# An attention and MLP kernel: for one unit per group, a DMA adds the first bit piece to the second, and one product per block falls away

## The chip, the core and the metric

The kernel runs on one core of one Trainium2 chip. The core has five engines with queues of their own, worked through in order: TensorE (PE, matmuls), ScalarE (ACT, activation functions), VectorE (DVE), GpSimd (POOL) and SyncE (SP, which issues DMAs). They meet through semaphores only. Data lie in SBUF and, for matmul results, in PSUM, each with 128 partitions; PSUM has eight banks of 512 fp32 values per partition. Sixteen DMA engines move data beside them.

The metric is device time in microseconds of one execution.

## The reference

```python
D, H, S, F = 640, 32, 2048, 1536                 # Dh = 20
xn = layernorm(x)
qkv = xn @ wqkv                                  # split into q, k, v of 32 heads
p = softmax(q @ k.T * Dh ** -0.5)                # 32 heads, 2048 x 2048 each
s = (p @ v) @ wo
h = gelu(layernorm(xn) @ w1)                     # then shifted by 1, -1, 2, -2 rows, by quarters of D
x1 = xn + shifted(h) @ w2
b = x1 + gelu(layernorm(x1) @ w3) @ w4
out = x + s * silu(b)
```

The costly part are the exponentials of the softmax: 32 heads of 2048 x 2048 scores, 134 million in all.

## The kernel before, in words

**Groups.** The 32 heads are worked in eight quads of four heads, and the 2048 queries in four chunks of 512: 32 groups (`attn_quad`). A group runs over 16 key tiles of 128 keys. For each key tile PE makes the scores of the four heads, two heads to a score tile of 128 keys x 1024 (two PSUM banks). Scores are made in one of two forms (`score_pair`): as row products, one matmul per head with four heads side by side in the rows of the array (line 1459), or as column products, four matmuls per head in the columns, over queries of one head with the other heads' rows at zero (line 1472). The planner decides the form of most tiles.

**Exponentials on two engines.** Most score tiles go through ACT (`exp_act`, line 1518), which writes the exponentials in bf16 into a tile of PT, a pool of 7. For the key tiles listed in `BLK`, half the score tiles take another way (`score_both`): DVE multiplies and adds (line 1540) so that the result, as a 16-bit integer, is the bit pattern of a rough exponential in bf16. It is kept in U, a pool of two buffers. One block is two key tiles, and its part in U is 2048 columns wide; a unit is one or two blocks, up to 4096 columns.

**Bit pieces.** `block_bits` refines that rough value. It takes the pattern four times, with 0, 32, 64 and 96 added to the integer (`EXP_B`): piece 0 is U itself, pieces 1 to 3 are written into SS, a pool of three buffers, by DVE (line 1442) or, for piece 3 of most units, by POOL (line 1440, a 32-bit integer add). PE multiplies all four with the values of the keys and adds up in PSUM (line 1451): one product of four matmuls per block and piece. Pieces 0 and 1 have weight 1 and take the values VA; pieces 2 and 3 have the weight 181/256 and take scaled values VP. The four matmuls of a product are one per head, with 22 columns of weights (20 values, a column of ones for the sum, one of zeros) and 512 queries.

The products of all key tiles of a group, those of PT (line 1312) and those of the pieces, add up in one PSUM bank. `ends` counts them, so that the first starts and the last ends the sum. DVE then takes the result out (line 1561), POOL normalises, and a transposing DMA and four more put it into HBM.

**Units.** `UNITS` says after which key tile of a group each unit's scores stand. Groups have two, four or five blocks (`ND`), so one to three units; the first unit of a group always holds blocks 0 and 1. The last of the 32 groups is made in another way (`last_half`) and has no such unit.

**What sets the order.** The program records tasks with the data that they read and write. The order of all of them, on all engines, is written out as one long string, `TABLE`: `follow` reads it, takes each task in turn onto its engine's queue, and gives out PSUM banks and PT tiles by the string's digits. It was made by a search elsewhere, with assumed durations; at run time only the order of each queue and the semaphores count. Tasks with `lock` are DVE operations in SBUF and POOL tasks; a POOL task waits for the last DVE task of that kind before it.

Everything else (projections of keys, queries and values, the MLP with its normalisations, the output projection) is fitted between the groups by the same string; its matmuls are mostly on line 684 (`mm_tile`).

Of the kernel before, what the change touches and what calls it, by code (L numbers as in the profile page):

```python
# [57 lines left out]
class Planner:  # L58
    def __init__(self):
# [15 lines left out]
        self.dma_lat0 = 1950.0  # L75
# [375 lines left out]
U8 = mybir.dt.uint8  # L451
# [15 lines left out]
class Cfg:  # L467
# [5 lines left out]
    def __init__(self, S=2048, D=640, H=32, F=1536):  # L473
# [34 lines left out]
        self.DT = False  # L508
        self.QS = False
# [46 lines left out]
        self.W7 = (0, 1)  # L556

# [56 lines left out]
class Gen:  # L614
# [76 lines left out]
    def build(self, plan_only=False):  # L691
        nc, pl = self.nc, self.pl
        with contextlib.ExitStack() as es:
# [12 lines left out]
                                for y in range(x + 1, 7) if x not in p and y not in p])  # L706
            pl.kind("SR", "B", [(2 * (k > 1), p + q) for k, p in enumerate(pairs) for q in pairs if not set(p) & set(q)])
# [95 lines left out]
    def alloc_persistent(self):  # L803
# [19 lines left out]
        self.PT = self.alloc("PT", [7, 1024], BF16)  # L823
# [36 lines left out]
    def load_inputs(self):  # L860
        cfg = self.cfg
        T, A = self.T, self.A
        X = self.xn
        xv = self.aps["A_x"][0].rearrange("(n p) d -> p n d", p=128)
        for n0 in range(0, cfg.NT, 2):
            n1 = n0 + 2
            T("sp", C_SP, lambda e, n0=n0, n1=n1: e.dma_start(X[:, n0:n1, :], xv[:, n0:n1, :]),
              writes=[A("xn", n) for n in range(n0, n1)], is_dma=True, nbytes=(n1 - n0) * 128 * cfg.D * 2,
              name=f"ld_x{n0}")
# [3 lines left out]
    def ln_tiles(self, tag, tiles, dst_of, dst_atoms_of, ve_out=None):  # L873
# [389 lines left out]
    def attn_quad(self, quad):  # L1263
# [9 lines left out]
        for qc in range(NQC):  # L1273
# [4 lines left out]
            if col:  # L1278
                T("sp", 2600, lambda e, qc=qc, gb=gb: [e.dma_start(self.QM[32 * i:32 * i + 32, gb, i, :],
                                                                 QT[32 * i:32 * i + 32, b, 512 * qc:512 * qc + 512]) for i in range(4)],  # L1280
                  reads=[A("QT", b, qc), A("QTa", b, qc)], writes=[A("QM", gb)], is_dma=True, nbytes=131072, name=f"qm{quad}_{qc}",
# [6 lines left out]
            done, total = [0], sum(5 if x[0] == "b" else 1 for x in seq)  # L1288
# [35 lines left out]
    def last_half(self, quad, qc, half, gb):  # L1324
# [40 lines left out]
        for x, kt in enumerate(ks):  # L1365
# [9 lines left out]
            for unit in at.get(x, []):  # L1375
# [3 lines left out]
                for m, kx in enumerate(unit):  # L1379
# [4 lines left out]
                      reads=[sa], writes=[A("U", ub, m)], name=f"uh{half}_{kx}", rel=hs, cls=-1 - half, due=self.at(self.nact, f"u{quad}"))  # L1384
                for v in range(4):
                    if v == 0:
                        dst, dsta = U[:, ub, :], [A("U", ub, m) for m in range(len(unit))]
                    else:
# [5 lines left out]
                          reads=[A("U", ub, m) for m in range(len(unit))], writes=dsta, name=f"s_h{half}_{unit[0]}_{v}", cls=-2 * half, lock=True,  # L1394
# [25 lines left out]
    def block_bits(self, quad, qc, blocks, ends):  # L1420
# [8 lines left out]
        halves = [A("U", ub, k) for k in range(2 * len(blocks))]  # L1429
        for v in range(4):  # L1430
# [13 lines left out]
            for n, (j, kts) in enumerate(blocks):  # L1444
# [17 lines left out]
    def score_pair(self, b, qc, kt, a, hs, sa, gb):  # L1462
        T, A = self.T, self.A
        me = []
        def fn(e):
            for jj in range(2):
                out = self.bank(hs.slots[jj])
# [3 lines left out]
                for c in range(4):  # L1471
# [5 lines left out]
                    writes=[sa], name=f"sc{self.tag}_{kt}_{a}", mode=int(gb is None), part=a + 1, flex=gb is not None, cls=-1, acq=("S", hs)))  # L1477
# [46 lines left out]
    def score_both(self, b, qc, kt, a, quad, r, gb):  # L1524
# [8 lines left out]
        (hs, sa), (hd, da) = self.stile(), self.stile()  # L1533
        for x, (h, ta) in ((a, (hs, sa)), (o, (hd, da))):
            self.score_pair(b, qc, kt, x, h, ta, gb)
        slot = self.exp_act(hs, sa, f"{self.tag}_{kt}_{a}")
        def fnu(e):
# [5 lines left out]
        T("dve", c_dve(1024), fnu, reads=[da], writes=[A("U", ub, at)], name=f"u{quad}_{qc}_{kt}", rel=hd,  # L1543
# [306 lines left out]
    def b_alloc3(self):  # L1850
# [6 lines left out]
        self.y3 = self.alloc("y3", [4, D], BF16)  # L1857
# [4 lines left out]
    def b_w34(self, c0):  # L1862
# [6 lines left out]
        for ch in (c0, c0 + 1):  # L1869
            i = ch % 2  # L1870
            tiles = list(range(4 * ch, 4 * ch + 4))
            tmp = self.ln_tiles(f"ln3_{ch}", tiles, lambda n, ch=ch: y3[:, n - 4 * ch, :], lambda n, ch=ch: [A("y3", n - 4 * ch)])
            self.free(*tmp)
            for bi, n in enumerate(tiles if cfg.DY else ()):
                T("sp", 1350, lambda e, bi=bi: e.dma_start_transpose(y3T[:, :, 128 * bi:128 * bi + 128], y3[:, bi, :]), reads=[A("y3", bi)],
                  writes=[A("y3T", bi)], is_dma=True, nbytes=163840, dlat=100.0, name=f"ty3_{n}", stream=f"ty{n % 4}")
            for kc in range(0 if cfg.DY else KC):
                self.transpose_w(f"y3_{ch}", kc, tiles, lambda n, ch=ch: y3[:, n - 4 * ch, :], lambda n, ch=ch: [A("y3", n - 4 * ch)],
# [16 lines left out]
        for hh in range(2):  # L1895
            hs = slice(hh * HALF, (hh + 1) * HALF)
            T("sp", C_SP, lambda e, hs=hs: e.dma_start(W4[:, :, :], w4src[:, :, hs]),
              writes=[A("W4")], is_dma=True, nbytes=FC * 128 * D, name=f"ld_w4_{c0}_{hh}", stream="w4")
# [19 lines left out]
    r"#9#0$R###%$G$$$^$<$,#(#&#,#6#:#'#;#<#)#$#*#-#i#a$&$-&J&K$.$%#`$'#y#v$(#u$)#x#=#w#>#b#.#?#t$/#@$0#z$1$*#A#{#B#|#_#m#j#d#k$+#n#C#l#o#}#D#E#p$3#F#f$_#G#H"  # L1918
    r"#q#I$K#J#~%((#K$I#L$L#g#M#N#O#P#Q$H$M$J#R#r#S#s$p#$z%${$|$k$$l$m$2$4$5$#%#&$6$N$7#c%$%%$O%&$A$u'$v$q$r$n$=$o#T$}$`$~$a$>$b$8$Q$@$w$x#e$V$?%'#U#V$y%7)$"
    r"s$t$;%-$#W$B$P$C$W#h#X#Y%_'%<#%`$S#Z#[$D%f&&I$c$E$e%D$9%g%=$d$F%2%%.$:%/%8%>%3%0$f%?$g%9%@%1%:%h%i%;%j$T$U%4%)%5%a%b%c$X$Y%6&L$&M(@&N&O%*%+&P&Q&b#&c%C"  # L1920
    r"$Z&d&e%,&f%m$%n#+$[%E%#]#^$]%d%Y'$h%J(%K$i%k%o%l%p%q%O)&g%F%G$j%H%T#%L#2#5%Z%M%I%P%U%N%[%V%]%A%W%^%X%Q%R%S%B%t&%u%v%r%s%w%x%y%{#%|%}%~%e&#&S(&T&U&$&%&"
    r"&&.$&V&W&/&'&0(A&)&X&,)&-&1&2&7#&8)}$&3%z)~#*#'*$&4&9**(*+%*&$*(*%#&:&;*,(&<*5$*')*1#*7(D&5#&6&(*-#*.*4(*2&*/$&Z&&[&]&^+$&o#16&_&p&`&q&r&s&t*6#*O(*0$*"
    r"9#*;*8$*3&@#&=&A&B&C*P(*H(*:$*J#&D']*)&E&i(&j&>)*D*I%&?&k&l&m*K)&n*]'&|$&}&~*^&*T$*M#*N',1*L'#'$'%&u#*U)&v&w*<&x&y*R#*d(*e%*Q'3('4'5&F&G)&z*='6'7*_'''"
# [118 lines left out]
```

## Time and profile before

| | |
|---|---|
| median of 3 runs | 804.62 us (802.0 to 806.14) |
| the profiled execution | 805.04 us, its span 803.3 us |
| PE busy | 777.6 us, 13680 matmuls |
| ACT busy | 766.8 us |
| DVE busy | 717.6 us |
| POOL busy | 328.5 us |
| DMA | 58.25 MB, 30.3% of the DMA engines' span for the main queue |
| granted TensorE clock | 0.99 |

Every line of the profile names a source line, an engine, an operation, the tiles (out<-in, all of them cut from one arena in SBUF, or psum), shape and count. Busy time and mean duration follow, then the idle time of the engine just before, with what ended it (the releaser). PE's busy time is the union of matmuls whose ends are modelled and overlap, so a busy PE is not a PE at its peak; what a matmul costs is better seen from how far apart starts are. PEld is PE's loading of weights, which runs ahead of the matmul. SPq is SP's queue of DMA issues. Stretches are given in us from the span's start.

### The profile page before, as it was taken

What the parts mean: (1) busy time and instruction counts of PE and PEld (TensorE: products, weight loads), DVE (VectorE), ACT (ScalarE), POOL (GpSimd) and SP (SyncE); (2) the same over time, 40 slices, a digit from 0 to 9 for tenths busy, and PEclk for the clock granted to TensorE, in tenths of its full rate; (3) what the DMA queues carried; (4) which work ended last, traced back from release to release, by engine and by line L of the source; (5) the groups of instructions that cost most, each with busy time, mean ns of one, the idle gap of its engine ahead of it and who ended that gap; (6) DMA issues with size and microseconds to landing.
All of it is one profiled execution on the core that took longest, in us unless ns stands there. A gap on an engine that the chain in (4) does not pass through costs nothing.

```text
span 803.3 us, 30126 instructions
## 1 busy us (share of the span) xinstructions
PE 777.6 (97%) x13680; PEld 329.5 (41%) x13680; DVE 717.6 (89%) x934; ACT 766.8 (95%) x796; POOL 328.5 (41%) x201
## 2 busy tenths in 40 slices
PE   7999999999999999999999999999998999999996
PEld 3443333334444433333534444334333444434574
DVE  7878899989999999998999899989888988888866
ACT  6899999999998999999999999999999999998995
POOL 5554334342426426344332453533423343444342
PEclk9999999999999999999999999999999999998998
DMA  5132433342213315423241132324232203123433
GB/s 176 31 107 61 130 90 73 78 90 55 52 20 62 54 45 110 85 57 82 67 109 31 34 84 61 67 52 83 55 91 51 50 14 85 27 62 115 100 103 100
DMA packets 141359, 58.25 MB, mean 73 GB/s; under 512 B 113728, under 2 KB 136432, under 8 KB 141232
## 3 DMA queue, kind: packets, MB, share of 16 engines
q1 hardware_dynamic: 141232, 56.33, 30.3%
q8 instruction: 107, 1.75, 0.9%
q14 instruction: 20, 0.16, 0.1%
HBM read 34.70 MB, written 10.33 MB: 56 GB/s over the span
## 4 chain that ended last, share of the span: by engine, by line
PE 48%; ACT 41%; DVE 8%; DMA 2%; SPq 0%; issue 0%; DVEq 0%
ACT arena L1518 35%; PE psum L684 16%; PE psum L1459 10%; PE psum L1451 8%; PE psum L1312 5%; PE psum L1472 5%; DVE arena L1540 3%; ACT arena L1892 3%; PE psum L1353 2%; DVE arena L1442 1%; DMA arena<-in_B_w_dram 1%; ACT arena L1818 1%; DVE arena L891 1%; DMA arena<-in_A_x_dram 1%; ACT arena L1908 1%; ACT arena L1500 1%
## 5 line engine op out<-in xcount | busy, mean ns | idle before, releaser
L1518 ACT ACTIVATE arena<-psum 128x1024 bf16<-128x1024 f32 x728 | 678.2, 1038 | 18.6 <-PE psum L1459 11.6
L1540 DVE TENSOR_SCALAR arena<-psum 128x1024 uint16<-128x1024 f32 x268 | 325.9, 1219 | 37.7 <-PE psum L1459 33.4
L684 PE MATMUL psum<-arena 128*32 128x320 bf16 (+1 forms) x5808 | 336.2, 332 | 1.7 <-DVE arena L1142 0.9
L1440 POOL TENSOR_TENSOR arena<-arena 128x2048 int32<-128x2048 int32 x61 | 219.6, 3600 | 284.1 <-DVE arena L1442 169.1
L1459 PE MATMUL psum<-arena 32*128 32x512 bf16 x1594 | 189.6, 385 | 10.6 <-ACT arena L1518 6.6
L684 PEld LDWEIGHTS psum<-arena 128*32 128x32 bf16 x5808 | 140.2, 96 | 124.8 <-issue 33.8
L1451 PE MATMUL psum<-arena 128*22 128x512 bf16 x2144 | 183.1, 382 | 0.0
L1442 DVE TENSOR_SCALAR arena<-arena 128x4096 uint16<-128x4096 uint16 (+1 forms) x158 | 170.5, 1100 | 2.2 <-PE psum L1451 1.4
L1312 PE MATMUL psum<-arena 128*22 128x512 bf16 x1448 | 137.9, 384 | 1.5 <-DVE arena L1561 1.3
L1459 PEld LDWEIGHTS psum<-arena 32*128 32x128 bf16 x1594 | 53.2, 91 | 174.0 <-ACT arena L1518 93.2
L1472 PE MATMUL psum<-arena 128*32 128x512 bf16 x1560 | 119.4, 382 | 0.7 <-ACT arena L1518 0.4
L1451 PEld LDWEIGHTS psum<-arena 128*22 128x22 bf16 x2144 | 50.0, 91 | 57.8 <-issue 23.0
L1569 POOL TENSOR_TENSOR arena<-arena 128x512 bf16<-128x512 f32 x30 | 40.9, 1365 | 58.5 <-DVE arena L1442 23.9
L1312 PEld LDWEIGHTS psum<-arena 128*22 128x22 bf16 x1448 | 35.5, 91 | 48.4 <-issue 21.9
L1472 PEld LDWEIGHTS psum<-arena 128*32 128x32 bf16 x1560 | 33.6, 95 | 41.7 <-ACT arena L1518 30.0
L1888 DVE CAST arena<-psum 128x512 bf16<-128x512 f32 x48 | 32.8, 683 | 4.6 <-PE psum L684 4.5
L1188 DVE CAST arena<-psum 128x512 bf16<-128x512 f32 x40 | 27.1, 683 | 1.8 <-PE psum L684 1.5
L891 DVE BATCH_NORM_STATS2 arena<-arena 128x6 f32<-128x320 bf16 x54 | 24.5, 480 | 3.1 <-DMA arena<-in_A_x_dram 3.1
L1730 POOL TENSOR_TENSOR arena<-arena 128x640 bf16<-128x640 bf16 x12 | 16.8, 1400 | 25.6 <-DVE arena L1668 20.0
L1668 DVE SCALAR_TENSOR_TENSOR arena<-psum,arena 128x320 bf16<-128x320 f32 x32 | 15.4, 487 | 11.7 <-PE psum L684 11.3
L1500 ACT ACTIVATE arena<-psum 128x2048 bf16<-128x2048 f32 x13 | 24.5, 1887 | 1.2 <-PE psum L1459 1.2
L1561 DVE STREAM_TRANSPOSE arena<-psum 128x512 f32<-128x512 f32 x31 | 22.1, 712 | 4.1 <-PE psum L1312 1.8
(120 smaller groups left out, 353.3 us busy)
## 6 DMA issues: line engine op xcount, KB each, us to landing
arena<-in_B_w_dram SPq DMA_DIRECT2D x48, 160.0 KB, 2.8
arena<-arena SPq DMA_DIRECT2D x124, 32.0 KB, 2.2
arena<-in_B_w_dram SPq DMA_DIRECT2D x4, 960.0 KB, 5.4
arena<-in_A_x_dram SPq DMA_DIRECT2D x8, 320.0 KB, 6.3
arena<-in_A_x_dram SPq DMA_DIRECT2D x16, 160.0 KB, 2.4
out_dram<-arena SPq DMA_DIRECT2D x16, 160.0 KB, 2.3
heads<-arena SPq DMA_DIRECT2D x120, 20.0 KB, 2.0
arena<-queries SPq DMA_DIRECT2D x28, 80.0 KB
```

The costliest lines, as they stand in the source:

```text
L684: ins = e.matmul(pb[32 * c:32 * c + 32, 0:N], lhsT(k, c), rhs(k, c), start=(k == 0), stop=(stop and k == nk - 1), tile_position=(0, 32 * c))
L891: lambda e, li=li, n=n, hh=hh: e.bn_stats(st[:, li, 6 * hh:6 * hh + 6], xn[:, n, hD * hh:hD * hh + hD]),
L1312: ins = e.matmul(pb[32 * i:32 * i + 22, 0:512], VA[:, ql, kts[i // 2], i, :], PT[:, slots[i // 2][0].slot, 512 * (i % 2):512 * (i % 2) + 512],
L1440: return e.tensor_tensor(dst.bitcast(I32), U[:, ub, 0:w].bitcast(I32), bass.AP(c.tensor, c.offset, [list(c.ap[0]), [0, w // 2]]), op=ALU.add)
L1442: fa if onp else lambda e, v=v, dst=dst: e.tensor_scalar(dst, U[:, ub, 0:w], EXP_B[v], None, op0=ALU.add),
L1451: ins = e.matmul(pb[32 * i:32 * i + 22, 0:512], wv, dst[:, at:at + 512].bitcast(BF16), start=first, stop=final, tile_position=(0, 32 * i))
L1459: return e.matmul(out, self.KT[32 * i:32 * i + 32, b, 128 * kt:128 * kt + 128], self.QT[32 * i:32 * i + 32, b, 512 * qc:512 * qc + 512], s ...
L1472: ins = e.matmul(out[32 * c:32 * c + 32, :], self.KT[:, b, 128 * kt + 32 * c:128 * kt + 32 * c + 32], self.QM[:, gb, 2 * a + jj, :], start ...
L1518: lambda e: e.activation(self.PT[:, hp.slot, :], self.psum[:, 512 * hs.slot:512 * hs.slot + 1024], AF.Exp, scale=cfg.scale),
L1540: ins = e.tensor_scalar(U[:, ub, 1024 * at + 512 * k:1024 * at + 512 * k + w], self.psum[:, 512 * hd.slots[k]:512 * hd.slots[k] + w], a_ex ...
L1569: return e.tensor_tensor(OnT.rearrange("p (k d a) -> p a k d", k=4, a=4), Ob[:, :].rearrange("p (a k d) -> p a k d", a=4, k=4), in1, op=AL ...
L1888: T("dve", c_dve(512), lambda e, h=h, fc=fc, i=i: e.tensor_copy(GT[:, i, fc, :], self.wbank(h)[:, 0:512]), reads=[wa], writes=at, name=f"g ...
```

## The change

For the first unit of each of 31 groups, the `acc` units of `ACC`, POOL issues a DMA that adds U (4096 columns of bf16 in 128 partitions, 1024 KB) onto piece 1 in SS, in SBUF. It waits for U and for piece 1, and the product of piece 1 waits for it. The products of piece 0 are left out for that unit, so three per block remain; `total` counts accordingly. Piece 1 of these units is made by DVE.

PT gets eight tiles instead of seven. The buffer y3 of the MLP's second normalisation holds two row tiles instead of four (`Y2`), and each tile's transposing DMA is recorded right behind its normalisation (`after`) instead of behind all four. The new kind "S2" and the option `US` are not used. Some assumed DMA durations (`dma_lat0`, `dlat`) differ, which changes no instruction. The string `TABLE` is new as a whole: the order of all queues and the choice of row or column form for some scores are others.

```diff
@@ Cfg
+        self.Y2 = True
+        self.NPT = 8
+        self.ACC = {(q, c): (0, 1) for q in range(8) for c in range(4)}
@@ alloc_persistent
-        self.PT = self.alloc("PT", [7, 1024], BF16)
+        self.PT = self.alloc("PT", [cfg.NPT, 1024], BF16)
@@ ln_tiles
                   reads=[A("xn", n), A(tag + "_rs"), A(tag + "_nb", li)], writes=dst_atoms_of(n), name=f"{tag}_norm{n}")
+                if after:
+                    after[li]()
                 continue
@@ attn_quad
-            done, total = [0], sum(5 if x[0] == "b" else 1 for x in seq)
+            done, total = [0], sum(5 - (x[1] in cfg.ACC.get((quad, qc), ())) if x[0] == "b" else 1 for x in seq)
@@ block_bits
-        halves = [A("U", ub, k) for k in range(2 * len(blocks))]
+        halves = [A("U", ub, k, x) for k in range(2 * len(blocks)) for x in range(2)]
+        acc = blocks[0][0] in cfg.ACC.get((quad, qc), ())
...
-            for n, (j, kts) in enumerate(blocks):
+            if acc and v == 1:
+                T("pool", 1000, lambda e, dst=dst: e.dma_start(dst.bitcast(BF16), U[:, ub, 0:w].bitcast(BF16), accum_op=ALU.add, max_dma_last_dim=4096),
+                  reads=halves + dsta, writes=dsta, is_dma=True, nbytes=2 * 256 * w, name=f"acc{quad}_{qc}_{blocks[0][0]}", stream="acc", lock=True)
+            for n, (j, kts) in enumerate([] if acc and v == 0 else blocks):
@@ b_alloc3
-        self.y3 = self.alloc("y3", [4, D], BF16)
+        self.y3 = self.alloc("y3", [2 if cfg.Y2 else 4, D], BF16)
@@ b_w34
-            tmp = self.ln_tiles(f"ln3_{ch}", tiles, lambda n, ch=ch: y3[:, n - 4 * ch, :], lambda n, ch=ch: [A("y3", n - 4 * ch)])
+            ny = 2 if cfg.Y2 else 4
+            yt = lambda n: y3[:, n % ny, :]
+            ya = lambda n: [A("y3", n % ny)]
+            turn = [lambda n=n: T("sp", 1350, lambda e: e.dma_start_transpose(y3T[:, :, 128 * (n % 4):128 * (n % 4) + 128], yt(n)), reads=ya(n),
+                                  writes=[A("y3T", n % 4)], is_dma=True, nbytes=163840, dlat=100.0, name=f"ty3_{n}", stream=f"ty{n % 4}") for n in tiles]
+            tmp = self.ln_tiles(f"ln3_{ch}", tiles, yt, ya, after=turn if cfg.DY else None)
-            for bi, n in enumerate(tiles if cfg.DY else ()):
-                T("sp", 1350, lambda e, bi=bi: e.dma_start_transpose(y3T[:, :, 128 * bi:128 * bi + 128], y3[:, bi, :]), reads=[A("y3", bi)],
-                  writes=[A("y3T", bi)], is_dma=True, nbytes=163840, dlat=100.0, name=f"ty3_{n}", stream=f"ty{n % 4}")
```

More of the change, by code (lines that the diff above doesn't have):

```diff
@@ L706, in build @@
                                 for y in range(x + 1, 7) if x not in p and y not in p])
+            pl.kind("S2", "B", [(2 * (k > 1), p) for k, p in enumerate(pairs)] + [(3, [i, j]) for i in range(7) for j in range(i + 2, 7)])
             pl.kind("SR", "B", [(2 * (k > 1), p + q) for k, p in enumerate(pairs) for q in pairs if not set(p) & set(q)])
@@ L1393, in last_half @@
                           lambda e, v=v, dst=dst, ub=ub, w=w: e.tensor_scalar(dst[:, 0:w], U[:, ub, 0:w], EXP_B[v], None, op0=ALU.add),
-                          reads=[A("U", ub, m) for m in range(len(unit))], writes=dsta, name=f"s_h{half}_{unit[0]}_{v}", cls=-2 * half, lock=True,
+                          reads=[A("U", ub, m, x) for m in range(len(unit)) for x in range(2)], writes=dsta, name=f"s_h{half}_{unit[0]}_{v}", cls=-2 * half, lock=True,
                           due=self.at(self.nact, f"s{quad}"))
```

215 lines of the change are left out of this document (114 added, 101 removed).

## The prediction

> **What bounds the kernel now.** I read the summary first, then the slices, the chain, the groups, the waits and a stretch of the timeline. Engine busy times, and ScalarE (ACT) by slices of 20 us:
>
> ```profile
> PE 777.6 (97%) x13680; PEld 329.5 (41%) x13680; DVE 717.6 (89%) x934; ACT 766.8 (95%) x796; POOL 328.5 (41%) x201
> ...
> ACT  6899999999998999999999999999999999998995
> ```
>
> Two engines look full. The stretch between prologue and tail (columns: PE, weight loads, DVE, ACT, POOL, then clock and DMA share) says how full:
>
> ```profile
> 40.00:780.00 740.00, 726.20 (x12470) 299.52 (x12466) 672.40 (x814) 723.41 (x735) 300.27 (x155) 1.00 0.31 70
> ```
>
> ACT idles 740.0 - 723.4 = 16.6 us in 740 (2.2%). Its instructions are the same in both kernels, so this is what the change can gain there. PE's busy time includes overlapping ends of matmuls; its real room shows in the starts:
>
> ```profile
> 399.36 20.32 ACT L1518 ACTIVATE arena<-psum 128x1024 bf16<-128x1024 f32 x22
> ...
> 400.91 0.60 PE L1451 MATMUL psum<-arena 128*22 128x512 bf16 x8
> ...
> 405.69 0.39 PE L1451 MATMUL psum<-arena 128*22 128x512 bf16 x4
> ...
> 413.47 0.39 PE L1459 MATMUL psum<-arena 32*128 32x512 bf16 x4
> ...
> 420.96 0.82 PE L1451 MATMUL psum<-arena 128*22 128x512 bf16 x12
> ```
>
> (Columns: start, duration, engine, line, count.) Four matmuls more cost (0.82 - 0.39) / 2 = 0.215 us: the price of one product. Four row scores (L1459) take the same 0.39, and some 0.1 more in the gap around them, say 0.43 us. One exponential costs 20.32 / 22 = 0.924 us, the beat of the kernel. The chain and the waits agree on who leads:
>
> ```profile
> PE 48%; ACT 41%; DVE 8%; DMA 2%; SPq 0%; issue 0%; DVEq 0%
> ...
> PEld psum L1459 <- ACT arena L1518: 93.2, 232, 1.0
> ...
> ACT arena L1518 <- PE psum L1459: 11.6, 31, 0.8
> ACT arena L1518 <- PE psum L1472: 3.3, 5, 1.1
> ```
>
> The score loads wait 93.2 us for ACT to free PSUM, ACT waits some 15 us for scores. The two alternate, and ACT leads.
>
> **What goes.** 31 units lose two products each: 62 x 0.215 = 13.3 us of PE. The order of the built program also has 96 fewer column-score matmuls (24 x 0.215 = 5.2 us) and 24 more row-score matmuls (6 x 0.43 = 2.6 us). Together PE loses 13.3 + 2.6 = 15.9 us, 0.43 us per 20 us of the middle. This helps only where ACT waits. In the 37 windows of 20 us from 40 to 780 us ACT idles 16.6 us; 12 windows idle over 0.43, and 11 not at all. Counting the smaller of the idle time and 0.43 in each gives 8.2 us. Bounds: 0 (the products sat in PE's waits) to 16.6 (saved time moves freely between windows). I take 8.2, since work is moved at most some groups apart. Prologue and tail: 0, bounded by 2 us either way, since the table is new there too.
>
> **What comes: 31 accumulating transfers.** No row shows one, nor any transfer issued by POOL. The rows nearest in size and place:
>
> ```profile
> arena<-in_B_w_dram SPq DMA_DIRECT2D x4, 960.0 KB, 5.4
> ...
> arena<-arena SPq DMA_DIRECT2D x124, 32.0 KB, 2.2
> ...
> heads<-arena SPq DMA_DIRECT2D x120, 20.0 KB, 2.0
> ```
>
> 20 KB land 2.0 us after issue, 960 KB 5.4 us after: a fixed 2.0 and 3.6 us per 1024 KB, the size of one accumulation. Low end: 2.0 + 3.6 = 5.6 us if the second operand is free. High end: 12.8, if both reads and the write pass one behind another. I take 9.2, two passes, because two operands have to be read. The rows include the issue, so POOL's is in it.
>
> In the Trainium skill, "Collectives: The Full Stack", section "The bandwidth ceiling: the fold count and why AG ≠ RS ≠ AR", the add in a DMA costs nothing by itself and the second source halves the rate. By that the price is near my 9.2; no run here shows it yet.
>
> **What covers it.** The sum is needed by the unit's first product, in PE's in-order queue; behind it stand scores, so ACT would starve. In the built order I counted, for each of the 31 units, the exponentials whose scores lie in PE's queue between the unit's last score and that product: 11, 12, 12, 13, 13, 14, 14, five of 15, four of 16, and 17 to 24 for the other 15. In that time pass the score (0.39), its conversion (L1540), the piece (L1442), three handoffs of 0.25 us, and the landing: 0.39 + 1.22 + 1.22 + 0.75 = 3.6 us and 9.2, so 12.8 us or 13.8 beats.
>
> ```profile
> L1540 DVE TENSOR_SCALAR arena<-psum 128x1024 uint16<-128x1024 f32 x268 | 325.9, 1219 | 37.7 <-PE psum L1459 33.4
> L1440 POOL TENSOR_TENSOR arena<-arena 128x2048 int32<-128x2048 int32 x61 | 219.6, 3600 | 284.1 <-DVE arena L1442 169.1
> L1442 DVE TENSOR_SCALAR arena<-arena 128x4096 uint16<-128x4096 uint16 x122 | 146.8, 1222 | 1.9 <-PE psum L1451 1.3
> ```
>
> Five units are short, by 7.6 us in all. ACT has about two score tiles in hand (2 x 0.924 = 1.85 us), so it loses only what exceeds that: 0.8 us. At 12.8 us 17 units are short by 52.4, and ACT loses 23.1; at 5.6 nothing. PE's saved 15.9 us must also refill the tiles, which it can: its loads wait 93.2 us.
>
> **The rest.** POOL waits in order for its piece before each accumulation; piece 3 (L1440, 3.6 us) stands behind that wait. POOL is busy 41%; 0, and if an accumulation stands behind a piece already running, 3.6 us, as if its landing were that much later. DVE and ACT keep their instructions: 0. The up-projection's transposes (16 on SP's queue) are now issued each behind its own normalise, with two buffers for four; a normalise can wait for a landing (2.8 us), eight times, in POOL's queue, where an accumulation can stand behind it. 0 to 8 x 2.8 = 22 us on POOL; 0 on the path, as POOL is idle 59%. One more PT tile lets ACT run a product longer ahead: 0, as ACT's listed waits are for scores. SP's queue carries nothing new, but its transfers share the DMA engines with 31 x 3.6 to 10.9 = 112 to 337 us of new data. Two waits for weights stand on the chain (3.5 and 6.4 us); 0, as they are issued that far ahead, up to 2 x 3.6 = 7.2. The piece buffers (three) and U (two) are held longer; a piece that waits for a buffer holds DVE, and behind it the conversions that free PSUM: 0, in the range.
>
> **Sum.** The profiled execution took 805.04 us (span 803.3 and 1.7 around), 0.4 over the median 804.62. 805.04 - 8.2 + 0.8 = 797.6 us.
>
> **A lock on POOL's descriptors.** The largest DVE group on SBUF alone (L1442) is busy 146.8 us at 1.22 us each; POOL's pieces last 3.6 us throughout, with 169.1 us of waits for that line, so the written order already keeps the two apart by waits. If each accumulation's issue nevertheless stands still for one such operation, landing is 10.4 us: 12 units short, ACT loses 4.4, time 805.04 - 8.2 + 4.4 = 801.2. For two operations (11.6) it loses 11.2: 808.0.
> The Trainium skill, "SBUF — State Buffer", names this under the "DVE blocks DMA" trap (SWDGE): GpSimd cannot write a DMA's descriptors while VectorE runs a two-port operation. By that rule the stall would be real; no transfer of POOL's is in this trace to say so.
>
> **Rivals.**
> - Forecast: covered landing, 797.6 us (788 to 800.6). For it: the beats counted. Chance 0.50.
> - No gain: the removed products only lengthen PE's waits for ACT, 805 us. For it: 11 windows without ACT idle, 93.2 us of waits. Against: ACT's 15 us waiting for scores. Chance 0.12.
> - The lock, 801.2 to 808.0 us. Chance 0.09, of which 0.06 within 0.5%.
> - Slower: the accumulation lands after its cover. PE stands at the first product, scores queue behind it, ACT starves. At 12.8 us: 805.04 - 8.2 + 23.1 = 819.9; without the gain 828. It is slower than before by over 0.5% when landing takes more than 11.8 us (a loss over 8.2 + 4). For it: no row shows such a transfer, and some land late for their size (the x loads, 320 KB in 6.3 us, where 2.0 + 1.1 would follow from it). Against: cover of 15 beats in the middle unit. Chance 0.25.
> - Held buffers or weights late by shared DMA engines: 7.2 to 20 us lost, 804 to 817. Chance 0.04, three quarters of it slower.
>
> **Numbers.** 0.5%, 4 us, is about what can be told from no change here. Faster (under 800.6): 0.50. Within: 0.12 + 0.06 + 0.01 = 0.19, and slower 0.25 + 0.03 + 0.03 = 0.31. Range: from 788.4 (all 16.6 gained) up to 825, between the slower case with and without the gain; about 0.15 is left above, for transfers slower than three passes, 0.03 below. If the forecast holds: 788 to 801.
>
> **What would show it.** 13,360 matmuls; L1451's count down by 248. ACT's idle time in the middle near 8 us. Accumulations landing in 8 to 10 us after issue. PE waits for DMA at the piece products under 10 us in all. A landing over 11.8 us, with PE waiting there 20 us or more, makes the forecast wrong; so does ACT's idle staying at 16 us with no such waits (no gain).

## The result

The changed kernel takes 825.6 us (median of 4 runs, 823.1 to 835.4) against 805.4 for the kernel before: 1.0278 of its time, 95% interval 1.0238 to 1.0318. It is slower by 20 us where 8 us of gain were forecast, and just above the range (825.0). The profiled execution took 824.5 us. The longest run, 835.4 us, had a granted clock of 0.981, the other three 0.986 to 0.993.

The summary of the changed kernel (span, busy times, ScalarE by slices, the chain by engine):

```profile
span 822.8 us, 29529 instructions
...
PE 781.7 (95%) x13360; PEld 322.1 (39%) x13360; DVE 719.4 (87%) x934; ACT 769.9 (94%) x796; POOL 370.6 (45%) x232
...
ACT  7899999989998899999999999999999999997895
...
ACT 46%; PE 38%; DVE 7%; DMA 6%; issue 1%; SPq 1%; POOL 1%; DVEq 0%
```

The 320 matmuls are gone as counted (13,680 to 13,360), yet PE is busy for longer than before. ACT's digits are 8 in the ninth and fourteenth slices, where they were 9 before, and lower near the end. Its stretch between prologue and tail:

```profile
40.00:800.00 760.00, 731.02 (x12140) 294.03 (x12137) 674.88 (x815) 725.29 (x734) 345.45 (x187) 0.99 0.56 109
```

ACT idles 760.0 - 725.3 = 34.7 us here; before it was 16.6. The waits of the changed kernel say that only a small part of it is PE standing for a sum:

```profile
PEld psum L1472 <- ACT arena L1532: 105.1, 254, 1.5
...
ACT arena L1532 <- PE psum L1472: 23.5, 42, 1.5
...
PEld psum L1464 <- DMA arena<-arena: 4.8, 4, 2.0
...
PE psum L1464 <- DMA arena<-arena: 2.9, 3, 1.7
```

(L1532 is the exponential, L1472 the row scores, L1464 the piece products.) The timeline has both rows at the same few places (166, 365 and 529 us; the fourth wait of the weight loads at 575 us): the loads, which run ahead, wait 4.8 us for the sums, PE itself 2.9. (My expectations below add the two to 7.7 us; that counts the same stops twice.) ACT's waits for row scores doubled, 11.6 to 23.5 us. The chain (start, length, what) passes through a sum in full three times, each from its issue to the instruction that waited for it:

```profile
154.77 11.40 DMA arena<-arena
...
353.90 10.76 DMA arena<-arena
...
519.02 10.28 DMA arena<-arena
```

PE's products wait for the first and the third; for the second it is DVE, which must not rewrite U before it has been read (two such waits, 1.4 us). These are late sums, 10.3 to 11.4 us from issue to use, where the median one lands in 8.8 us (below). All these waits together are a few us, so most of the loss has another source.

### The profile page after: what moved, and what is told of

Read it like the earlier page. It is cut to its first block, busy times and chain, and to the rows that moved or that the text cites. A ratio compares the mean times of both kernels' runs of the same rounds, so it can differ in the third digit from the quotient of the medians.

```text
span 822.8 us, 29529 instructions
## 1 busy us (share of the span) xinstructions
PE 781.7 (95%) x13360; PEld 322.1 (39%) x13360; DVE 719.4 (87%) x934; ACT 769.9 (94%) x796; POOL 370.6 (45%) x232
## 4 chain that ended last, share of the span: by engine, by line
ACT 46%; PE 38%; DVE 7%; DMA 6%; issue 1%; SPq 1%; POOL 1%; DVEq 0%
ACT arena L1532 39%; PE psum L690 13%; PE psum L1472 9%; PE psum L1464 5%; DMA arena<-arena 4%; PE psum L1321 4%; PE psum L1485 3%; DVE arena L1563 3%; ACT arena L1917 3%; ACT arena L1514 2%; PE psum L1362 2%; DVE arena L1452 1%; ACT arena L1841 1%; DVE arena L898 1%; DMA keys<-arena 1%
## 5 line engine op out<-in xcount | busy, mean ns | idle before, releaser
L1532 ACT ACTIVATE arena<-psum 128x1024 bf16<-128x1024 f32 x728 | 681.8, 1037 | 35.0 <-PE psum L1472 23.5
L1450 POOL TENSOR_TENSOR arena<-arena 128x2048 int32<-128x2048 int32 x61 | 226.4, 3711 | 173.4 <-DVE arena L1452 113.4
L1472 PE MATMUL psum<-arena 32*128 32x512 bf16 x1618 | 209.5, 386 | 19.7 <-ACT arena L1532 10.0
L690 PEld LDWEIGHTS psum<-arena 128*32 128x32 bf16 x5808 | 141.6, 96 | 124.2 <-issue 35.0
L1452 DVE TENSOR_SCALAR arena<-arena 128x4096 uint16<-128x4096 uint16 (+1 forms) x158 | 174.1, 1114 | 7.4 <-PE psum L1464 6.4
L1464 PE MATMUL psum<-arena 128*22 128x512 bf16 x1896 | 160.7, 381 | 3.6 <-DMA arena<-arena 2.9
L1321 PE MATMUL psum<-arena 128*22 128x512 bf16 x1448 | 136.6, 383 | 3.5 <-DVE arena L1584 2.8
L1472 PEld LDWEIGHTS psum<-arena 32*128 32x128 bf16 x1618 | 56.9, 91 | 196.4 <-ACT arena L1532 105.1
L1485 PE MATMUL psum<-arena 128*32 128x512 bf16 x1464 | 111.9, 382 | 1.0 <-ACT arena L1532 0.6
L1455 POOL DMA_DIRECT2D arena<-arena x31 | 41.0, 1322 | 110.9 <-DVE arena L1452 105.5
L1464 PEld LDWEIGHTS psum<-arena 128*22 128x22 bf16 x1896 | 44.1, 91 | 61.8 <-issue 25.0
L1321 PEld LDWEIGHTS psum<-arena 128*22 128x22 bf16 x1448 | 35.3, 91 | 49.8 <-issue 19.6
L1485 PEld LDWEIGHTS psum<-arena 128*32 128x32 bf16 x1464 | 30.3, 95 | 40.3 <-ACT arena L1532 27.7
L1691 DVE SCALAR_TENSOR_TENSOR arena<-psum,arena 128x320 bf16<-128x320 f32 x32 | 15.5, 488 | 20.2 <-PE psum L690 19.9
L898 DVE BATCH_NORM_STATS2 arena<-arena 128x6 f32<-128x320 bf16 x54 | 23.7, 478 | 1.1 <-DMA arena<-in_A_x_dram 1.1
```

The source lines that it names most:

```text
L690: ins = e.matmul(pb[32 * c:32 * c + 32, 0:N], lhsT(k, c), rhs(k, c), start=(k == 0), stop=(stop and k == nk - 1), tile_position=(0, 32 * c))
L1321: ins = e.matmul(pb[32 * i:32 * i + 22, 0:512], VA[:, ql, kts[i // 2], i, :], PT[:, slots[i // 2][0].slot, 512 * (i % 2):512 * (i % 2) + 512],
L1450: return e.tensor_tensor(dst.bitcast(I32), U[:, ub, 0:w].bitcast(I32), bass.AP(c.tensor, c.offset, [list(c.ap[0]), [0, w // 2]]), op=ALU.add)
L1452: fa if onp else lambda e, v=v, dst=dst: e.tensor_scalar(dst, U[:, ub, 0:w], EXP_B[v], None, op0=ALU.add),
L1455: T("pool", 1000, lambda e, dst=dst: e.dma_start(dst.bitcast(BF16), U[:, ub, 0:w].bitcast(BF16), accum_op=ALU.add, max_dma_last_dim=4096), ...
L1464: ins = e.matmul(pb[32 * i:32 * i + 22, 0:512], wv, dst[:, at:at + 512].bitcast(BF16), start=first, stop=final, tile_position=(0, 32 * i))
```

## The experiments

### Transfers, products or order?

Two kernels take the transfers out of the changed kernel; one of them puts the products of piece 0 back. What then differs from the kernel before is the order, the eighth PT tile and the smaller y3.

```diff
@@ block_bits, without the transfers
-            if acc and v == 1:
-                T("pool", 1000, lambda e, dst=dst: e.dma_start(..., accum_op=ALU.add, ...), ...)
@@ Cfg, four products: this too, and 62 products set into the order
-        self.ACC = {(q, c): (0, 1) for q in range(8) for c in range(4)}
```

> The changed kernel with the 31 accumulating transfers taken out and nothing else; piece 0's share of those 31 units is missing from the output. Every queue keeps the changed kernel's order. Three theories. Waiting: the loss comes from PE standing at the first product until the sum has landed; then without the transfers the time is my forecast without its landing term, 797 us, within 795 to 803. Sharing: the loss comes from the data of the transfers (31 x 1024 KB) slowing SP's transfers and holding U and the pieces longer; here the same, 795 to 803. Order: the new order of the queues itself runs worse on the chip than the old one, whatever the transfers do; then only PE's direct waits for them go, 7.7 us in the trace (4.8 at the weight loads, 2.9 at the matmuls), and the time is 815 to 822 us.

> The changed kernel's order with the transfers taken out and the products of piece 0 put back, each ahead of the first of its block's other products; the whole function is computed, and PE has the 62 products (13.3 us at 0.215 each) again. It differs from the kernel before by the order, the eighth PT tile and the two y3 buffers. Waiting and sharing: a time near the kernel before, 800 to 812 us (797 plus at most 13.3). Order: slower than the changed kernel without the transfers by up to 13.3 us, 820 to 833 us.

Without the transfers: 818.3 us (1.0154, 1.0128 to 1.0181). With four products: 827.1 us (1.0270, 1.0233 to 1.0307). So the loss comes with order and buffers, and the account of the change is, in us:

| step | time |
|---|---|
| before | 805.3 |
| new order and buffers, four products, no transfers | 827.1 (+21.8) |
| 62 products removed | 818.3 (-8.8) |
| transfers added: the change | 825.6 (+7.3) |

### What are the products worth in the old order?

```diff
@@ before, attn_quad and block_bits; the 62 products leave the string, all else keeps its place
-            done, total = [0], sum(5 if x[0] == "b" else 1 for x in seq)
+            done, total = [0], sum(5 - (x[1] in cfg.ACC.get((quad, qc), ())) if x[0] == "b" else 1 for x in seq)
...
-            for n, (j, kts) in enumerate(blocks):
+            for n, (j, kts) in enumerate([] if acc and v == 0 else blocks):
```

> The kernel before in its own order, with the 62 products of piece 0 left out in the first unit of 31 groups and no transfer in their place; piece 0's share of those units is missing from the output. PE loses 13.3 us, and the row and column scores stay as they were. If my term for the gain holds in the old order, 8.2 us or a little less of the idle time of ScalarE goes: 796 to 800 us. If the products sat in PE's waits: 803 to 806.

803.9 us, 0.9969 of the kernel before (0.9951 to 0.9988): 1 to 4 us, not 8. The stretch that I had read for the gain, now without the products:

```profile
40.00:780.00 740.00, 721.53 (x12252) 294.02 (x12256) 670.63 (x812) 723.64 (x736) 299.01 (x156) 1.00 0.31 70
```

ACT idles 740.0 - 723.6 = 16.4 us, as before (16.6). None of the idle time that was to be won has gone. Even a sum that cost nothing would have been worth a few us at most here.

### The transfers: landing, size, source

Three edits of the transfer in the changed kernel: half the columns; a copy in place of a sum; a sum into a scratch tensor in HBM that no product waits for.

```diff
@@ half the columns
-e.dma_start(dst.bitcast(BF16), U[:, ub, 0:w].bitcast(BF16), accum_op=ALU.add, max_dma_last_dim=4096)
+e.dma_start(dst[:, 0:w // 2].bitcast(BF16), U[:, ub, 0:w // 2].bitcast(BF16), accum_op=ALU.add, max_dma_last_dim=4096)
@@ plain copy
+e.dma_start(dst.bitcast(BF16), U[:, ub, 0:w].bitcast(BF16), max_dma_last_dim=4096)
@@ into scratch
+e.dma_start(self.dz, U[:, ub, 0:w].bitcast(BF16), accum_op=ALU.add, max_dma_last_dim=4096)
-                  reads=halves + dsta, writes=dsta, ...
+                  reads=halves + dsta, writes=[("dz",)], ...
```

> The changed kernel's order, with the 31 transfers issued from the same place in POOL's queue, of the same size and read from the same U, but added into a scratch tensor in HBM that nobody reads; so no product waits for them, and piece 0's share of the 31 units is missing from the output. U is still held until the transfer has read it. Waiting: as without the transfers, 795 to 803 us. Sharing: nearly the changed kernel's time less its 7.7 us of direct waits, 815 to 822 us. Order: the same 815 to 822, but then the kernel without the transfers is equally slow, which tells the two apart.

> The changed kernel with each accumulating transfer covering only the first 2048 of 4096 columns, 512 KB instead of 1024; the second block's piece 0 is missing from the output. The landing was 8.8 us after issue at the median, 1.8 of it before the first packet; half the data should land at 1.8 + 3.5 = 5.3 us. Waiting: most of the loss goes, 800 to 808 us. Sharing: about half of it goes, 808 to 815. Order: only part of the 7.7 us of direct waits goes, 817 to 824.

> The changed kernel with the 31 transfers made plain copies: U is copied over piece 1 with the same size, queue, order and waits, so one source is read in place of two, and piece 1's share of those units is missing from the output. The sum landed 8.8 us after its issue at the median (1.8 to the first packet, 6.9 of data). If the second source halves the rate, as my 9.2 us had it (two passes of 3.6), the copy lands 3.5 us earlier, near 5.3 us, and the time falls by about what half the data saved, to 819 to 822 us. If the addition costs the transfer nothing, it lands in 8 to 9.5 us and the time stays at 823 to 827.

| kernel | us | ratio (95%) |
|---|---|---|
| no transfers | 818.3 | 1.0154 (1.0128 to 1.0181) |
| half sums | 819.5 | 1.0169 (1.0144 to 1.0195) |
| plain copies | 817.3 | 1.0156 (1.0127 to 1.0184) |
| sums into scratch | 822.2 | 1.0210 (1.0188 to 1.0231) |
| sums: the change | 825.6 | 1.0278 (1.0238 to 1.0318) |

The landings, from the DMA issues of the plain copy:

```profile
arena<-arena POOLq DMA_DIRECT2D x31, 1024.0 KB, 5.5
```

and of the half sums:

```profile
arena<-arena POOLq DMA_DIRECT2D x31, 512.0 KB, 5.3
```

For the full sum the page has no time to landing. The records of its packets have the first start 1.8 us after the issue and the last end after 8.8 at the median (7.9 to 10.9). By the same records the copy's first packet starts after 1.4 us and its last ends after 5.0; the 5.5 above is some 0.45 more, until the landing is noted. So the data of the copy take 3.3 us at the median and those of the sum 6.7, for the same 1024 KB. The Trainium skill ("Collectives: The Full Stack", "The bandwidth ceiling: the fold count and why AG ≠ RS ≠ AR") says of a collective's reduce step that the add is free and the second source halves the rate. The trace agrees for this transfer, 3.3 against 6.7 us.

What landed within 5.5 us cost nothing that can be measured, copy and half sum alike. The full sum, 3.8 us later by the packets, cost 7.3 us. With the sums into scratch, for which no product waits, 3.9 us are lost. The chain of that kernel shows where:

```profile
154.71 12.29 DMA dz<-arena
...
474.87 8.00 DMA arena<-in_B_w_dram
...
646.83 10.45 DMA dz<-arena
```

Twice the chain passes through the transfer itself, as U must not be rewritten before it has been read; once through a weight load of 8.0 us. In this kernel the weight loads of 960 KB land 6.7 us after their issue and those of 160 KB 3.3, against 5.6 and 2.7 without the transfers. I have not told the two shares apart. Nor is the 3.9 shown to be a part of the 7.3: these sums go to HBM, and in the changed kernel the same weight loads land after 5.8 and 3.2 us.

### Pairs of row scores

The new order has 12 score tiles more in row form and fewer neighbours of different head pairs. I took this for a cause. A tile's two halves can be exchanged in the order without moving anything:

```diff
@@ TABLE, one of the exchanged key tiles, as tasks
- sc0_0_13_1 exp0_0_13_1 ... sc0_0_13_0 ... exp0_0_13_0
+ sc0_0_13_0 exp0_0_13_0 ... sc0_0_13_1 ... exp0_0_13_1
```

> Row scores of the two head pairs share the array: four matmuls of a (1, 2) pair of tiles take 0.39 us, but two tiles of the same head pair in a row take 0.39 each. Counted over the built orders, the row scores need 470 such steps of 0.39 us before and 509 after. This kernel is the changed kernel, transfers and all, in which 67 key tiles have the places of their two score tiles (and of their two exponentials) exchanged in the order; every position, buffer and wait is otherwise as it was, and 34 steps fall away: 475, so 34 x 0.39 = 13.3 us of PE. The whole function is computed. Pairing: the lost pairs are a main cause of the slower order; 13.3 us of PE were worth 8.8 us with the products, so 812 to 819 us. Placement: what costs is where the order puts the work (ScalarE idles more from 240 to 320 us and from 740 us to the end), the pairs sit in PE's waits elsewhere; 822 to 826 us.

> The kernel before, in which 47 key tiles have the places of their two score tiles exchanged in the order so that the row scores need 509 steps of 0.39 us in place of 470, as in the changed kernel: 15.2 us more of PE, nothing else moved. The whole function is computed. Pairing: 811 to 820 us (0.4 to 1 us for each us of PE). Placement: 804 to 808 us.

> The kernel before, in which 49 key tiles have the places of their two score tiles exchanged so that the row scores need 452 steps in place of 470: 18 x 0.39 = 7.0 us less of PE, nothing else moved. The whole function is computed. Pairing: 799 to 803 us. Placement: 804 to 807.

The changed kernel with 34 steps fewer: 829.1 us (1.0276, 1.0236 to 1.0316), no gain. The kernel before with 39 steps more: 812.2 (1.0086, 1.0055 to 1.0117), 7 us slower; with 18 fewer: 806.6 (1.0014, 0.9998 to 1.0030), no gain. Both forecasts for the changed kernel (812 to 819, 822 to 826) were missed. The theory falls: pairs are not what makes the new order slow. The three runs show something else. In the old order, 15 us more of PE's work, as counted, cost 7 us, and 7 or 13 us less gained nothing or 1 to 4.

### Is there room for a sum in the old order?

```diff
@@ TABLE, unit 0 of group (4, 1), as tasks, with the transfer of block_bits
  s4_1_0_2 s4_1_0_1
- pvd4_1_1_0 pvd4_1_1_1 s4_1_0_3 pvd4_1_1_2 pvd4_1_0_1 pvd4_1_0_0 pvd4_1_0_2 pvd4_1_1_3 pvd4_1_0_3
+ acc4_1_0 s4_1_0_3 pvd4_1_1_2 pvd4_1_0_1 pvd4_1_1_1 pvd4_1_0_2 pvd4_1_1_3 pvd4_1_0_3
```

> The kernel before with the transfers and nothing else of the change: old order, old buffers (four y3, seven PT tiles), 62 products of piece 0 gone, POOL issues the sum right behind piece 1, and piece 1's products stand as late as the old order lets them: at the unit's last product, or just before the task that writes their buffer next. The whole function is computed. Counted in that order, 1 to 14 exponentials lie between piece 1 and that place (median 8), and 11.7 are needed (piece 1.22, hand-over 0.25, sum landed and seen by TensorE 9.3, over 0.924 us). If the old order has no room for the sum: 120 us of shortage, 74 less the two score tiles in hand, so 875 us or more, above all if other queues wait behind. If the new order wasn't needed for the sum: 805 to 815.

965.9 us (two runs), 1.1997 of the kernel before. Here PE does wait for the sums (L1456 the products, L1464 the row scores, L1523 the exponential):

```profile
ACT arena L1523 <- PE psum L1464: 99.2, 64, 8.8
...
PEld psum L1456 <- DMA arena<-arena: 86.3, 20, 8.4
PE psum L1456 <- DMA arena<-arena: 77.8, 20, 7.9
```

Its weight loads stop for them 20 times, 86 us in all, against four times and 4.8 us in the changed kernel. That is not all of the 161 us lost. The granted clock is 0.92 here, against 0.99 in the kernel before: the trace has it at half for 153 us in 24 stretches, before 17 us in three. My estimate from these is up to 68 us lost that way, half of what was added. The sum needs an order made for it. That is what the new string gives; new order and new buffers together cost the 21.8 us.

### Where does the new order lose?

The traces give the start of the transpose that takes each group's sums out of PSUM. Its lag behind the kernel before, in us, after group (quad, chunk); the padded kernels come below:

| group | four products, new order | no transfers | after | old order, new buffers | the same, padded | old start, padded |
|---|---|---|---|---|---|---|
| 1, 1 | +2.4 | +1.8 | +1.8 | -1.2 | -0.9 | -1.4 |
| 2, 0 | +5.4 | +4.0 | +4.2 | -1.2 | -0.9 | -1.2 |
| 2, 1 | +10.0 | +8.2 | +8.8 | +8.8 | -0.9 | -1.2 |
| 3, 0 | +11.9 | +11.5 | +11.5 | +8.8 | -0.8 | +3.9 |
| 3, 1 | +14.6 | +14.0 | +15.1 | +12.7 | +4.4 | +6.6 |
| 4, 2 | +14.6 | +12.5 | +13.9 | +18.2 | +10.9 | +6.5 |
| 5, 2 | +15.2 | +11.8 | +15.5 | +25.4 | +18.3 | +7.1 |
| 7, 2 | +19.9 | +14.8 | +19.4 | +26.7 | +19.1 | +13.4 |

The three kernels with the new order lose alike, transfers or not, and most of it between (1, 1) and (3, 1). That is where the second MLP half begins, with its normalisations, y3, and the up-projection. So I tested the middle of the new order alone, and the new buffers alone:

```diff
@@ TABLE: the new order in the middle
+ old order to ob1_1 | what the new order has up to ob5_2 | what is left, in the old order
@@ Cfg on the old order: the buffers (four products, no transfers), with this order of a chunk's tasks
+        self.Y2 = True
+        self.NPT = 8
- ln3_0_norm3 ln3_0_norm2 ln3_0_norm1 ln3_0_norm0 ty3_0 ty3_2 ty3_3 ... ty3_1
+ ln3_0_norm0 ty3_0 ln3_0_norm1 ty3_1 ln3_0_norm2 ty3_2 ln3_0_norm3 ty3_3
```

> All four products, no transfers, the whole function. The old order (with two y3 buffers) up to the end of the sixth group, the changed kernel's order from there to the end of the twenty-third, the old one again after it. Counted from the ends of the groups in the traces, the new order with four products is 2.4 us behind the old after six groups, 14.6 after fourteen, 15.2 after twenty-three and 19.9 at the last. Place: the loss is made in the middle by the order there, so 805 + 12.8 = 818 us, within 814 to 822. Spread: if the loss is carried in from the start (other buffers free, other work left over) or paid at the end, the middle alone costs little; 804 to 811 us.

> The kernel before (all four products, no transfers, the whole function) with the change's buffers alone: eight PT tiles and two y3 buffers. TensorE and ScalarE keep the old order instruction by instruction. As two row tiles now share a y3 buffer, the four normalisations of a chunk are put in rising order on POOL and each transposing transfer right behind its own, and 17 small tasks of POOL and the first chunk's statistics on DVE stand a little later. Order alone: the buffers cost nothing by themselves, the new string is what is slow; 804 to 808 us. Buffers: a normalisation has to wait until the transpose of two tiles earlier has landed, and that one until the up-projection has read the chunk before, so normalisations can't run a chunk ahead, and the old order stalls on it; 815 us or more. Then the new order would be what the search had to give up for the eighth PT tile.

The new middle: 824.3 us (1.0233, 1.0207 to 1.0260), nearly the whole loss, and 2 us above the range for it (814 to 822). The new buffers in the old order: 834.3 us (1.0359, 1.0328 to 1.0391), slower than the change itself, though TensorE and ScalarE keep their order. From group to group it loses in four steps, 10.0, 3.9, 6.1 and 7.2 us, one at each chunk of the second half. The chain of this kernel at the first chunk (L914 the normalisation, L1449 a piece on POOL, L1460 the piece products):

```profile
271.61 0.90 POOL arena L914 x2
272.51 2.62 DMA arena<-arena
...
275.21 0.88 POOL arena L914
...
276.54 0.87 POOL arena L914
277.42 3.58 POOL arena L1449
...
281.04 0.64 PE psum L1460 x8
```

Two normalisations, then the wait for a transpose to land (2.62 us), then the other two, and behind them in POOL's queue the piece that PE waits for. This is the wait that the prediction had named and set to 0 on the path.

Each step has a second part. PE stands still at the four places for 7.0, 2.5, 4.2 and 6.3 us (from 266, 347, 482 and 558 us). Within 5 us of each stop's start the granted clock falls to half, for 6.8, 3.4, 3.4 and 6.8 us. The first of these stretches (PE, weight loads, DVE, ACT, POOL, then clock and DMA):

```profile
271.00:277.80 6.80, 4.33 (x36) 1.13 (x36) 5.14 (x8) 2.09 (x3) 4.17 (x6) 0.50 0.31 63
```

In all the clock is at half for 35 us here, against 17 in the kernel before. My estimate from these two, half of what was added: up to 9 of the 29 us are lost behind the stops and not in them.

### A buffer in the wrong place

At the first chunk there is one thing more. y3 is 2,560 bytes shorter, so what is allocated behind it has moved down by that much against the tile hx of the first MLP half, whose space it reuses. The small statistics buffer of the chunk lay 2,048 bytes behind hx; now it lies in hx's last 512. So each of the chunk's statistics has to wait until the down-projection has read hx for the last time. The timeline of DVE shows it. The kernel before (L891 statistics, L1846 an addition of the down-projection):

```profile
233.34 0.48 DVE L1846 TENSOR_TENSOR arena<-psum,arena 128x320 bf16<-128x320 f32 x1
233.73 0.48 DVE L891 BATCH_NORM_STATS2 arena<-arena 128x6 f32<-128x320 bf16 x1
...
269.71 0.47 DVE L1846 TENSOR_TENSOR arena<-psum,arena 128x320 bf16<-128x320 f32 x1
```

The changed kernel (L898 and L1869):

```profile
266.76 0.96 DVE L1869 TENSOR_TENSOR arena<-psum,arena 128x320 bf16<-128x320 f32 x2
267.64 3.24 DVE L898 BATCH_NORM_STATS2 arena<-arena 128x6 f32<-128x320 bf16 x8
```

Before, the first statistic runs at 233.7 us, 36 us ahead of the last addition. Now all eight run in one row at 267.6 us. In the new string the first of them is the very next task behind the last matmul of the down-projection; in the old string it stands some 420 tasks ahead of it. Four kernels test this with a line of padding:

```diff
@@ b_alloc3
         self.TH = self.alloc("TH", [2, D], BF16)
+        self.pad = self.alloc("pad", [256], BF16)
```

It goes into the old order with the new buffers; into the changed kernel; and into two kernels that run the old order up to the end of group (2, 1) and the new one from there, without and with the sums:

```diff
@@ TABLE: old start
+ old order to ob2_1 | what is left, in the new order
@@ Cfg, with the sums
+        self.ACC = {(q, c): (0, 1) for q in range(8) for c in range(4) if 4 * q + c > 9}
```

> The old order with the new buffers (834.3 us), plus 512 bytes of padding behind TH, so that the statistics buffer of the first chunk lies behind the place of hx (the first MLP's hidden tile) and no longer inside it. In the changed kernel each statistic of that chunk waits for 162 earlier tasks, all of the down-projection among them; in the kernel before and here for one, its own row tile. Four products, no transfers, the whole function. Layout: the 10 us lost at the first chunk go, and the 17 us of the other three chunks (4.0, 6.1 and 7.2) stay: 824 us, within 820 to 827. Two y3 buffers alone: 831 to 836.

> The changed kernel with the same 512 bytes of padding and nothing else: the same order on every queue, the same transfers. If the first chunk's statistics wait in this order for the down-projection at run time, the wait goes: 815 to 819 us. If the order was made around it and has these tasks late in the queues anyway, nothing moves: 823 to 827 us.

> The old order up to the end of the tenth group (2, 1), the changed kernel's order from there, with the new buffers and the padding; four products, no transfers, the whole function. The new order with four products (827.1 us) was 10.0 us behind the old at that group's end. If its loss is made in this stretch: 817 us, within 815 to 820. If the new order from there on depends on its own start, or pays later anyway: 823 us or more.

> As the run with the old start, but with the transfers and three products in the 21 units after the tenth group; the ten units before keep four products. The whole function is computed. Against the changed kernel (825.6 us) 8.8 us at the tenth group's end and the products of ten units (10/31 of 8.8 = 2.8 us lost) and their transfers (10/31 of 7.3 = 2.4 us won): 817 us, within 813 to 820. If the transfers cost more in these groups than the products are worth: above 820. Below 805 it would beat both kernels, which nothing measured so far promises.

| kernel | us | ratio (95%) |
|---|---|---|
| old order, new buffers, padded | 824.9 | 1.0239 (1.0221 to 1.0256) |
| after, padded | 829.3 | 1.0295 (1.0275 to 1.0316) |
| old start, four products, padded | 818.6 | 1.0164 (1.0146 to 1.0181) |
| old start, sums from (2, 2) on, padded | 821.7 | 1.0211 (1.0169 to 1.0253) |

In the old order more than the line differs: with the padding DVE's queue is again that of the kernel before, statistics included, which without it had to stand behind the down-projection. This gives 9.4 of the 29 us back: the step at (2, 1) is gone (table, +8.8 to -0.9), though the two y3 buffers are still there, and the other three remain (5.2, 6.5 and 7.4). These come with the two y3 buffers and the order of normalisations, pieces and transposes that was set for them on POOL and SP; no run has one without the other, or the eighth PT tile alone. At the second chunk the chain of the padded kernel is (L1895 the transposes, L1905 a weight load of the up-projection, both in SP's queue):

```profile
328.20 2.62 DMA arena<-arena
...
330.91 4.04 POOL arena L914 x2
...
335.35 1.27 SPq L1895
...
336.67 0.58 SPq L1905
...
337.30 2.84 DMA arena<-in_B_w_dram
```

A normalisation waits for a transpose, the next transposes wait for the normalisations in SP's queue, and the weights that PE needs are issued behind them.

In the changed kernel the padding alone gives nothing (829.3 us, above the 823 to 827 that I expected of no effect): its order has these tasks late in the queues anyway. The old start in front of the new order gives 827.1 - 818.6 = 8.5 us. So 8 to 10 us of the new order's 21.8 are lost before the end of group (2, 1), and with the padding the same buffers allow an order that loses none there. That the overlap put them there is not tried by itself, as it would take another search, but they stand at the first place that it allows. The other 13 us fall later, in pieces (table, last column); how much of them the y3 buffers force and how much the room for the sums, no run here tells, as none has the new order with the old buffers. The old start with the sums, 821.7 us where 813 to 820 were expected, can't be told from the changed kernel (the intervals overlap), and no version that computes the whole function beats the kernel before.

## Why the prediction was wrong

**What bounds the kernel.** That ACT leads and PE is close behind held for the old order: more work on PE cost 7 us for 15, less gained little.

**The gain, 8.2 us.** The step "counting the smaller of the idle time and 0.43 in each" window failed. In the old order the products are worth 1 to 4 us, with ACT's idle time unmoved (16.4 us after 16.6). That a window has ACT idle does not say that the saved matmuls lay ahead of the late score there; which they lay ahead of, no run shows. The "no gain" rival described this better. That the new order has 8.8 us is no confirmation; that order gave ACT the idle time first.

**The 2.6 us for scores in other forms.** No run has this change by itself, so the term stays open. The count of matmuls said a gain of 2.6; by the count of steps the row scores cost 15 us more, and 34 steps less moved no time.

**The landing, 9.2 us.** This held, and so did its reason, two passes: the last packet ended 8.8 us after the issue, so PE could start after some 9.3, and a copy of the same size landed in 5.5, where one pass was put at 5.6. So did the cover: five units short by 7.6 us on paper, four waits of 4.8 us in the trace. The price did not: "ACT loses 0.8", but the transfers cost 7.3. The direct waits for sums on record are 4.8 us at PE's weight loads and 1.4 at DVE for U. The term for held buffers and shared DMA engines, which I had set to 0 with bounds up to 7.2, is not nothing: sums that no product waits for cost 3.9, though into HBM. How the 7.3 divide stays open.

**The rest, 0.** Here is the step that decided. "0 on the path, as POOL is idle 59%" for the two y3 buffers took an idle share for cover. The normalisations stand in POOL's queue ahead of a piece, the transposes in SP's queue ahead of weights, and in the old order this costs 29 us, 9.4 of it by a buffer that moved into the place of another, and up to 9 (an estimate) at the halved clock behind the stops. And "prologue and tail: 0, bounded by 2 us either way" was all that I allowed for a string that is new as a whole. I costed the instructions that changed and took the quality of the order as given; it cost 21.8 us with the buffers. None of the rivals was a worse order.

**The rivals.** The time of the slower rival, 819.9 to 828, came true, but not its mechanism: it decided at a landing over 11.8 us, and the longest was 10.9 after the issue, 11.4 until the product. So it is luck that the time lies in that rival's range, and only 0.6 us above mine. The lock on descriptors stays open: POOL's issue took 1.3 us on average and the first packet left 3.3 us after it at the latest, but the program lets each issue wait for DVE's last operation in SBUF, so the case doesn't arise cleanly.

## What to carry to other kernels

When a change comes with a new order of all queues, the order can be the larger part of the change, here 21.8 us with the buffers against -8.8 and +7.3: compare where each stage's tasks stand in it, and not only how many instructions fall away. A buffer made smaller to pay for another moves everything allocated behind it; look at what each of those now overlaps, since a new overlap is a wait that no line of the diff shows. Busy time saved on the second-busiest engine is not worth the first one's idle time in the same windows: here 8.2 us were counted that way and 1 to 4 came.

## What the runs showed of the hardware

A DMA that adds 1024 KB of bf16 from SBUF onto SBUF took twice as long for its data as a copy, 6.7 against 3.3 us, and its last packet ended 8.8 us after the issue against 5.0. The copy cost nothing that can be measured, the sum 7.3 us in all. The sum also costs POOL more to issue, 1.32 us on average against 0.80 for the copy.

A stop of PE cost more than its length: in the old order with the new buffers, stops of 7.0, 2.5, 4.2 and 6.3 us stand at steps of 10.0, 3.9, 6.1 and 7.2. In that kernel and in the old order with the sums, every stop of 2 us or more after the prologue (4 and 20 of them) was followed within 5 us of its start by 3.4 to 10.2 us at half the granted clock. Such stretches also occur without a stop, at 723 us in the kernel before.
